# A Fourier mixing layer and a maxout layer: the 96-point stage of batches 2 to 7 as two 48-point ones

## The chip, the cores and the metric

The kernel runs on one core of a Trainium2 chip. A core has five engines with instruction queues of their own: TensorE (matrix products; PE in the profile, its weight loads PEld), VectorE (DVE), ScalarE (ACT), GpSimd (POOL) and SyncE (SP, which here only issues transfers). Sixteen DMA engines move data between device memory, SBUF (on-chip, 128 partitions) and nothing else; TensorE writes to PSUM, from which VectorE and ScalarE copy. The metric is the device time of one execution in microseconds (us); less is better.

## The reference

```python
def _attn_ref(x, filt_r, filt_i):              # x: 8 x 3072 x 256, float32
    X = np.fft.rfft(x, axis=1)
    F = (filt_r + 1j * filt_i)[None, :, :]     # 1537 x 256
    Y = X * F
    y = np.fft.irfft(Y, n=x.shape[1], axis=1)
    return y.astype(np.float32)

def _moe_ref(x, w1, w2, w_out):                # 24576 tokens, 256 -> 1024 -> 256
    h1 = x @ w1
    h2 = x @ w2
    g = np.maximum(h1, h2)
    return (g @ w_out).astype(np.float32)
```

The second function is applied to the first one's output, with batch and sequence flattened.

## The kernel before

**The transform.** The 3072 points of a batch are taken as 96 rows (p) of 32 (m). Stage one, `f1` (L277), is a 96-point real transform over the rows: TensorE multiplies the table `C1` (96x96) with `x` for two values of m at a time (512 columns), ScalarE copies the result `pa` from PSUM to a tile `at` (L285), and every second call SP writes `at` to device memory `ad` (L287). `f1_read` (L289) reads `ad` back in another layout as `bt`, in two halves by frequency group. Stage two is made in *visits* (L333): visit n multiplies four groups with 64x64 tables `U` (`s2`, L301, results `px`), VectorE multiplies `px` by the filter `F` (`product`, L310, result `pq`, two of them per visit), and the next visit takes `pq` back through 64x64 tables `VP` and `VQ` (`s3`, L316, results `pz`), which ScalarE copies to `zt` (L327) and SP writes to device memory `zd` (L328). A batch has seven visits: the first has only `s2`, the last only `s3`. The 64x64 tables use the array as four tiles: two row halves by two column halves. `z_read` (L295) reads `zd` back as `zr` in two halves. `s4` (L342) is the 96-point inverse, which gives `y`, 384 tokens at a time; ScalarE and VectorE copy one `py` each.

**The maxout layer.** max(h1, h2) is computed as h2 + relu(h1 - h2): `Wd` = w1 - w2 and `M` = w2 w_out are made at the start. For a tile of 384 tokens, `moe_h` (L361) makes one of eight blocks `ph` of the hidden layer, whose relu goes to `gt` by ScalarE (L371) or VectorE (L369), and `moe_o` (L382) makes three or four matmuls of the output of the tile before it, `po`. VectorE copies two finished `po` to `ot` (L406) and Pool issues the output transfers (L380).

**The order.** The whole order is written out by hand: each engine executes its instructions in the order in which the program issues them. After a start section (batch 0's transform, weights, tables) the main loop runs over 65 tiles with eight steps each, so 64 steps are one batch of output. A step is `moe_h`, then three or four matmuls of `moe_o`, then what was planned for this step, in the order of the `plan` calls (L562). After step 4 of a tile (6 in the last of a batch) comes `s4` of the next tile. While batch b's output is made, the visits of batch b + 1 run (`plan_f2`, L570), `f1` of batch b + 2 (`plan_f1`, L565, every third step) and the loads of x for batch b + 3 (`plan_x`, L576). While batch 0's output is made, `f1` of both batch 1 (steps 4 to 19) and batch 2 (20 to 27, 54 to 61) run, and batch 1's visits stand at steps 28, 32, 36, 39, 42, 46 and 49.

**Buffers.** All results of `f1`, `s2`, `s3`, `s4` and `moe_h` go through one PSUM tag, `ps`, with six buffers (L66) that are handed out in strict turn: a new tile waits until the tile six before it has been read. `po` has a tag of its own with two. `bt` and `zr` have two buffers, `at` four (of four m each), x sixteen.

**Queues.** Pool loads x with a cast to bf16 (`load_x`, L75) and issues the output transfers. SP issues `ad`, `bt`, `zd` and `zr`. Each queue executes in order, and a transfer whose data is not ready holds those behind it.

Of the kernel before, what the change touches and what calls it, by code (L numbers as in the profile page):

```python
# [8 lines left out]
FP32 = mybir.dt.float32  # L9
BF16 = mybir.dt.bfloat16  # L10
AF = mybir.ActivationFunctionType
OP = mybir.AluOpType

B = 8
N = 3072
D = 256
HID = 1024
NP = 96
NM = 32
NW = 12  # L20
NU = 24
# [5 lines left out]
def kernel(  # L27
# [14 lines left out]
    nc = tc.nc  # L42
    V, S, G, TE = nc.vector, nc.scalar, nc.gpsimd, nc.tensor

    const = ctx.enter_context(tc.tile_pool(name="const", bufs=1))
    C1 = const.tile([NP, 96], BF16)
# [13 lines left out]
    w2T = const.tile([128, 8, D], BF16)  # L60

    dram = ctx.enter_context(tc.tile_pool(name="dram", bufs=2, space=bass.MemoryType.DRAM))
    xpool = ctx.enter_context(tc.tile_pool(name="xpool", bufs=16))
    bpool = ctx.enter_context(tc.tile_pool(name="bpool", bufs=2))
    pqpool = ctx.enter_context(tc.tile_pool(name="pqpool", bufs=6))
    ps = ctx.enter_context(tc.tile_pool(name="ps", bufs=6, space=bass.MemoryType.PSUM))  # L66
# [6 lines left out]
    xb = {}  # L73

    def load_x(b, c):  # L75
        t_ = xpool.tile([NP, 4, D], BF16, tag="xb", name="xb")
        src = x[b].rearrange("(p m) d -> p m d", m=NM)
        G.dma_start(out=t_, in_=src[:, 4 * c:4 * c + 4, :])  # L78
        xb[b, c] = t_

    def load_f(h):
# [63 lines left out]
    def table_c():  # L145
        p96 = init.tile([128, 1], FP32)
        V.tensor_scalar(p96, pid, 1.0 / 96.0, None, OP.mult)
        uc = init.tile([NP, 48, 2], FP32)
        rc = init.tile([NP, 48, 2], FP32)
        kf = kc.rearrange("p w g s -> p (w g s)")  # L150
        V.tensor_scalar(uc[:, :, 0], kf, p96[0:NP], 0.25, OP.mult, OP.add)
        V.tensor_scalar(uc[:, :, 1], kf, p96[0:NP], None, OP.mult)
        V.tensor_scalar(uc[:, 0:1, 1], pid[0:NP], 0.5, 0.25, OP.mult, OP.add)
        V.tensor_scalar(rc, uc, RND, RND, OP.add, OP.subtract)
        V.tensor_tensor(uc, uc, rc, OP.subtract)
        S.activation(C1, uc.rearrange("p k r -> p (k r)"), AF.Sin, bias=zero[0:NP], scale=TWO_PI)

    ua = init.tile([128, NU, 2, 2, 16], FP32)
    ru = init.tile([128, NW, 64], FP32)
# [111 lines left out]
    bt = {}  # L271
    zr = {}
    ad = {}
    zd = {}
    at_ = {}

    def f1(b, c):  # L277
        if c == 0:
            ad[b] = dram.tile([96, NM, D], BF16, tag="ad", name="ad")
        if c % 2 == 0:  # L280
            at_[b] = apool.tile([96, 4, D], BF16, tag="at", name="at")
        at = at_[b]
        pa = ps.tile([96, 2, D], FP32, tag="ps", name="pa")
        TE.matmul(pa, C1, xb[b, c // 2][:, 2 * (c % 2):2 * (c % 2) + 2], start=True, stop=True)  # L284
        S.activation(at[:, 2 * (c % 2):2 * (c % 2) + 2], pa, AF.Copy)  # L285
        if c % 2 == 1:
            nc.sync.dma_start(out=ad[b][:, 2 * c - 2:2 * c + 2], in_=at)  # L287

    def f1_read(b):  # L289
        bt[b] = bpool.tile([128, NU, D], BF16, tag="bt", name="bt")  # L290
        for h in range(2):
            src = ad[b].rearrange("(u q) m d -> (q m) u d", q=4)[:, 12 * h:12 * h + 12]
            nc.sync.dma_start(out=bt[b][:, 12 * h:12 * h + 12], in_=src)

    def z_read(b, h):  # L295
        if h == 0:
            zr[b] = zrpool.tile([96, NM, D], BF16, tag="zr", name="zr")
        nc.sync.dma_start(out=zr[b][48 * h:48 * h + 48],
                          in_=zd[b][12 * h:12 * h + 12].rearrange("u (q m) d -> (u q) m d", q=4))

    def s2(b, v):  # L301
        px = [ps.tile([128, 2, D], FP32, tag="ps", name="px%d" % s) for s in range(2)]
        for i in range(2):
            for s, g in ((0, 0), (1, 1), (0, 1), (1, 0)):
                u = 2 * (2 * v + i) + g
                TE.matmul(px[s][64 * g:64 * g + 64, i], U[64 * s:64 * s + 64, u], bt[b][64 * s:64 * s + 64, u],  # L306
                          start=True, stop=True)
        return px

    def product(E, v, s, px):  # L310
        pq = pqpool.tile([128, 2, 2, D], BF16, tag="pq", name="pq")
        E.tensor_tensor(pq, px.rearrange("p (o i) d -> p o i d", o=1).to_broadcast([128, 2, 2, D]),  # L312
                        F[:, :, 2 * v:2 * v + 2, s], OP.mult)
        return pq

    def s3(b, v, pq):  # L316
        if v == 0:
            zd[b] = dram.tile([NU, 128, D], BF16, tag="zd", name="zd")
        pz = [ps.tile([128, 2, D], FP32, tag="ps", name="pz%d" % g) for g in range(2)]
        for i in range(2):  # L320
            for q, tab in enumerate((VP, VQ)):
                for g, s in ((0, 0), (1, 1), (0, 1), (1, 0)):
                    TE.matmul(pz[g][64 * s:64 * s + 64, i], tab[64 * g:64 * g + 64, 2 * v + i, s],  # L323
                              pq[s][64 * g:64 * g + 64, q, i], start=(q == 0), stop=(q == 1))
        zt = zpool.tile([128, 2, 2, D], BF16, tag="zt", name="zt")
        for g in range(2):
            S.activation(zt[:, :, g], pz[g], AF.Copy)  # L327
        nc.sync.dma_start(out=zd[b][4 * v:4 * v + 4].rearrange("u p d -> p u d"),  # L328
                          in_=zt.rearrange("p i g d -> p (i g) d"))

    pend = {}

    def visit(b, n):  # L333
        if n > 0:
            s3(b, n - 1, pend.pop((b, n - 1)))
        if n < 6:
            px = s2(b, n)
            pend[b, n] = [product(V, n, s, px[s]) for s in range(2)]

    yt = {}  # L340
# [20 lines left out]
    def moe_h(tt, j):  # L361
        if j == 0:
            gt[tt] = gpool.tile([128, 8, 384], BF16, tag="gt", name="gt")
        y_ = yt[tt]
        ph = ps.tile([128, 384], FP32, tag="ps", name="ph")
        for dc in range(2):
            TE.matmul(ph, Wd[:, dc, 128 * j:128 * j + 128], y_[:, dc], start=(dc == 0), stop=(dc == 1))  # L367
        if (tt, j) in on_v if tt < 8 else j in (1, 3, 6):
            V.tensor_scalar(gt[tt][:, j], ph, 0.0, None, OP.max)  # L369
        else:  # L370
            S.activation(gt[tt][:, j], ph, AF.Relu)  # L371
# [106 lines left out]


    table_c()  # L480
    V.tensor_scalar(I128, cid, pid, None, OP.is_equal)
    V.tensor_scalar(NI, cid, pid, -1.0, OP.is_equal, OP.mult)
# [65 lines left out]
    t2(0, (V, S))  # L548
    spin(2)
    setup.close()  # L550
    apool = ctx.enter_context(tc.tile_pool(name="apool", bufs=4))
    zpool = ctx.enter_context(tc.tile_pool(name="zpool", bufs=3))
    ypool = ctx.enter_context(tc.tile_pool(name="ypool", bufs=3))
    gpool = ctx.enter_context(tc.tile_pool(name="gpool", bufs=2))
# [7 lines left out]
    def plan(b, step, fn, *a):  # L562
        todo.setdefault((b + step // 64, step % 64), []).append((fn, a))

    def plan_f1(b, nb, steps, read):  # L565
        for c, n in zip(range(16), steps):
            plan(b, n, f1, nb, c)
        plan(b, read, f1_read, nb)

    def plan_f2(b, nb, steps, z0, z1):  # L570
        for n, st in zip(range(7), steps):
            plan(b, st, visit, nb, n)
        plan(b, z0, z_read, nb, 0)
        plan(b, z1, z_read, nb, 1)

    def plan_x(b, nb, steps):  # L576
        for c, n in zip(range(8), steps):
            plan(b, n, load_x, nb, c)

    plan(0, 2, t2, 1, (V,))  # L580
    plan(0, 5, prep_t, 0)
    plan(0, 6, prep_t, 1)
    plan(0, 7, prep_m)
    for c in range(2, 8):
        plan(0, 8 * (c - 2) + 8, t2, c, (V,))
    plan_x(0, 2, range(2, 10))
    plan_f1(0, 1, range(4, 20), 20)
    plan_f2(0, 1, (28, 32, 36, 39, 42, 46, 49), 41, 51)
    plan_f1(0, 2, list(range(20, 28)) + list(range(54, 62)), 62)
    plan_x(0, 3, range(54, 102, 6))  # L590
    for b in range(1, B):
        if b + 2 < B:
            plan_f1(b, b + 2, range(1, 64, 3), 54)
        if b + 3 < B:
            plan_x(b, b + 3, range(8, 64, 7))
        if b + 1 < B:
            plan_f2(b, b + 1, range(8, 50, 6) if b == 1 else range(6, 48, 6), 33 if b == 1 else 32, 50 if b == 1 else 49)

    for tt in range(8 * B + 1):
        b, i = divmod(tt, 8)  # L600
        k = 0
        for j in range(8):
            step = 8 * i + j
            if tt < 8 * B:
                moe_h(tt, j)
            if tt > 0:
                n = 3 if j in (3, 7) else 4
                moe_o(tt - 1, k, k + n)
                k += n
            for fn, a in todo.get((b, step), ()):  # L610
                fn(*a)
            if j == (4 if i < 7 else 6) and tt + 1 < 8 * B:
                s4(tt + 1)
# [30 lines left out]
```

## Time and profile before

| what | us |
|---|---|
| three runs, median (lowest, highest) | 519.16 (518.43, 519.32) |
| the profiled execution, its own time | 519.43 |
| its span (first to last instruction) | 517.5 |
| TensorE busy in it (5212 matmuls) | 500.9 |
| VectorE / ScalarE / Pool busy | 325.4 / 313.2 / 165.1 |
| granted TensorE clock, mean | 0.99 |

The costliest groups that the text speaks of (line, engine, operation, out<-in, shape, count, then busy us and mean ns of one; behind the bar the engine's idle time before them and what ended most of it):

```profile
L285 ACT ACTIVATE at<-pa 96x512 bf16<-96x512 f32 x112 | 66.4, 593 | 30.0 <-PE pa L284 27.3
L284 PE MATMUL pa<-xb,C 96*96 96x512 bf16 x112 | 42.7, 382 | 0.7 <-DMA xb<-in_x_dram 0.7
L78 POOL DMA_DIRECT2D xb<-in_x_dram x64 | 33.9, 536 | 5.4 <-DMA xb<-in_x_dram 4.3
L323 PE MATMUL pz<-pq,VP 64*64 64x256 bf16 x336 | 21.9, 281 | 0.0
L306 PE MATMUL px<-bt,U 64*64 64x256 bf16 x384 | 20.0, 278 | 0.2
```

And the transfers (KB each, median us from issue to landing):

```profile
xb<-in_x_dram POOLq DMA_DIRECT2D x64, 192.0 KB, 5.8
ad<-at SPq DMA_DIRECT2D x56, 192.0 KB, 3.5
bt<-ad SPq DMA_DIRECT2D x14, 768.0 KB, 8.6
zd<-zt SPq DMA_DIRECT2D x42, 256.0 KB, 3.5
zr<-zd SPq DMA_DIRECT2D x14, 768.0 KB, 7.7
w1f<-in_moe_w_dram SPq DMA_DIRECT2D x2, 512.0 KB, 5.3
```

A matmul's modelled length holds the latency of the pipeline (382 ns for a pa of 512 columns), so lengths of neighbours overlap and the busy time of a group is more than it adds; the distance from one start to the next is what an instruction takes. Idle time of an engine that is not the bottleneck costs nothing.

### The profile page before, as it was taken

The page shows a single profiled execution, that of the slowest core. Times are in us where ns is not written, and L with a number is a line of the kernel's source. Part 1 is how long each engine was busy: PE and PEld are TensorE (multiplying, and loading weights), DVE is VectorE, ACT ScalarE, POOL GpSimd, SP SyncE. Part 2 cuts the span into 40 slices and gives each one's busy share as a digit, 9 for nine tenths or more (in the row PEclk, how much of TensorE's full clock was granted, in tenths as well). Part 3 has the DMA queues.
Part 4 walks back from the last instruction along what each step waited for, and adds up shares of the span by engine and source line. Part 5 has one row for each costly group of instructions (what it writes and reads, how often), then busy time and mean ns, then how long its engine had stood idle before and what let it go on. Part 6 is the DMA issues. An engine that isn't in the chain of part 4 may idle for free.

```text
span 517.5 us, 12635 instructions
## 1 busy us (share of the span) xinstructions
PE 500.9 (97%) x5212; PEld 364.3 (70%) x5212; DVE 325.4 (63%) x503; ACT 313.2 (61%) x636; POOL 165.1 (32%) x289
## 2 busy tenths in 40 slices
PE   7678999999999999999999999999999999999997
PEld 3445777777777777777777777777777777777775
DVE  7673558547774577547764677557774687554543
ACT  6655667766774577656675576646765455544442
POOL 6887212224323232332323233231222122222220
PEclk9879999999999999999999999999999999999999
DMA  7979973879798577874699577892377426521112
GB/s 124 167 208 179 248 240 127 196 228 246 189 227 239 173 169 162 242 229 119 159 215 230 156 169 176 216 258 96 133 186 195 151 100 146 153 84 72 62 62 82
DMA packets 72635, 88.12 MB, mean 170 GB/s; under 512 B 6561, under 2 KB 52898, under 8 KB 71906
## 3 DMA queue, kind: packets, MB, share of 16 engines
q1 hardware_dynamic: 53218, 47.72, 34.3%
q0 software_dynamic: 19360, 39.60, 31.5%
q8 instruction: 41, 0.67, 0.5%
q14 instruction: 16, 0.13, 0.1%
HBM read 54.53 MB, written 47.19 MB: 197 GB/s over the span
## 4 chain that ended last, share of the span: by engine, by line
PE 89%; DMA 5%; POOL 3%; ACT 1%; DVE 1%; issue 0%; SPq 0%; POOLq 0%
PE ph L367 33%; PE po L394 32%; PE po L392 8%; PE pa L284 5%; PE pz L323 5%; PE py L348 4%; DMA xb<-in_x_dram 2%; PE px L306 2%; DMA w1f<-in_moe_w_dram 1%; DMA F<-in_filt_i_dram 1%; POOL Wd L252 1%; POOL xb L78 1%; POOL F L90 1%; POOL F L87 1%; PE pr L467 1%; DVE pq L312 0%
## 5 line engine op out<-in xcount | busy, mean ns | idle before, releaser
L394 PE MATMUL po<-Wo,gt 128*128 128x256 bf16 x1536 | 260.6, 272 | 0.0
L371 ACT ACTIVATE gt<-ph 128x384 bf16<-128x384 f32 x323 | 157.4, 490 | 117.0 <-PE ph L367 116.0
L380 POOL DMA_DIRECT2D out_dram<-ot x186 | 102.0, 553 | 329.8 <-DVE ot L406 321.0
L394 PEld LDWEIGHTS <-gt 128*128 128x128 bf16 x1536 | 149.7, 97 | 61.7
L369 DVE TENSOR_SCALAR gt<-ph 128x384 bf16<-128x384 f32 x189 | 104.0, 554 | 71.9 <-PE ph L367 65.2
L312 DVE TENSOR_TENSOR pq<-px,F 128x1024 bf16<-128x1024 f32 x92 | 108.4, 1220 | 39.6 <-PE px L306 34.5
L367 PEld LDWEIGHTS <-Wd 128*128 128x128 bf16 x1024 | 94.5, 98 | 29.0 <-issue 7.9
L285 ACT ACTIVATE at<-pa 96x512 bf16<-96x512 f32 x112 | 66.4, 593 | 30.0 <-PE pa L284 27.3
L406 DVE COPY ot<-po 128x512 f32<-128x512 f32 x95 | 65.3, 687 | 30.4 <-PE po L394 29.3
L327 ACT ACTIVATE zt<-pz 128x512 bf16<-128x512 f32 x84 | 45.6, 594 | 24.6 <-PE pz L323 24.6
L284 PE MATMUL pa<-xb,C 96*96 96x512 bf16 x112 | 42.7, 382 | 0.7 <-DMA xb<-in_x_dram 0.7
L78 POOL DMA_DIRECT2D xb<-in_x_dram x64 | 33.9, 536 | 5.4 <-DMA xb<-in_x_dram 4.3
L348 PE MATMUL py<-G,zr 96*128 96x96 bf16 x512 | 32.6, 206 | 0.2
L348 PEld LDWEIGHTS <-zr 96*128 96x128 bf16 x512 | 27.7, 98 | 6.1 <-issue 3.1
L323 PE MATMUL pz<-pq,VP 64*64 64x256 bf16 x336 | 21.9, 281 | 0.0
L323 PE MATMUL pz<-pq,VQ 64*64 64x256 bf16 x336 | 20.9, 269 | 0.0
L306 PE MATMUL px<-bt,U 64*64 64x256 bf16 x384 | 20.0, 278 | 0.2
L323 PEld LDWEIGHTS <-VP 64*64 64x64 bf16 x336 | 9.7, 105 | 8.7 <-issue 8.4
L284 PEld LDWEIGHTS <-C 96*96 96x96 bf16 x112 | 13.8, 123 | 2.3 <-DMA xb<-in_x_dram 1.1
L477 PE MATMUL pd<-W 128*128 128x512 bf16 x33 | 11.0, 448 | 1.8 <-DVE zero L123 1.5
L306 PEld LDWEIGHTS <-U 64*64 64x64 bf16 x384 | 10.2, 108 | 2.5 <-issue 2.3
L323 PEld LDWEIGHTS <-VQ 64*64 64x64 bf16 x336 | 9.8, 107 | 0.0
(419 smaller groups left out, 568.3 us busy)
## 6 DMA issues: line engine op xcount, KB each, us to landing
out_dram<-ot POOLq DMA_DIRECT2D x186, 128.0 KB, 2.8
xb<-in_x_dram POOLq DMA_DIRECT2D x64, 192.0 KB, 5.8
ad<-at SPq DMA_DIRECT2D x56, 192.0 KB, 3.5
bt<-ad SPq DMA_DIRECT2D x14, 768.0 KB, 8.6
zd<-zt SPq DMA_DIRECT2D x42, 256.0 KB, 3.5
zr<-zd SPq DMA_DIRECT2D x14, 768.0 KB, 7.7
w1f<-in_moe_w_dram SPq DMA_DIRECT2D x2, 512.0 KB, 5.3
w2f<-in_moe_w_dram SPq DMA_DIRECT2D x2, 512.0 KB, 5.8
```

Source lines behind the costliest of these rows:

```text
L284: TE.matmul(pa, C1, xb[b, c // 2][:, 2 * (c % 2):2 * (c % 2) + 2], start=True, stop=True)
L285: S.activation(at[:, 2 * (c % 2):2 * (c % 2) + 2], pa, AF.Copy)
L312: E.tensor_tensor(pq, px.rearrange("p (o i) d -> p o i d", o=1).to_broadcast([128, 2, 2, D]), F[:, :, 2 * v:2 * v + 2, s], OP.mult)
L323: TE.matmul(pz[g][64 * s:64 * s + 64, i], tab[64 * g:64 * g + 64, 2 * v + i, s], pq[s][64 * g:64 * g + 64, q, i], start=(q == 0), stop=(q ...
L327: S.activation(zt[:, :, g], pz[g], AF.Copy)
L348: TE.matmul(py[:, m], zr[b][:, 4 * i + m, 128 * dc:128 * dc + 128], G1, start=True, stop=True)
L367: TE.matmul(ph, Wd[:, dc, 128 * j:128 * j + 128], y_[:, dc], start=(dc == 0), stop=(dc == 1))
L369: V.tensor_scalar(gt[tt][:, j], ph, 0.0, None, OP.max)
L371: S.activation(gt[tt][:, j], ph, AF.Relu)
L380: E.dma_start(out=dst, in_=ot[tt // 2][:, 3 * (tt % 2) + c])
L394: TE.matmul(p_, g_[:, n - 2, blk], Wo[:, n - 2], start=False, stop=(n == 9))
L406: V.tensor_copy(ot[tt // 2][:, e - 1:e + 1], po[0])
```

## The change

From batch 2 on, stage one is split by the parity of the rows' upper half: with rows p and p + 48 added and subtracted, the 96-point transform becomes a 48-point one of the sums (even frequencies) and one of the differences (odd ones). SP loads x as it is, float32, with rows p and p + 48 side by side on 48 partitions, two m on partitions 0 to 47 and two on 64 to 111 (`load_xf`). Pool makes sums and differences of a quad of four m (`fold`), in bf16. TensorE multiplies them with `CT`, two 64x64 tables on each half of the partitions, as four 64x64 matmuls of 512 columns (`s1`), and ScalarE copies two tiles of 128x512. The `at` tile holds eight m, so there are two writes of 192 KB per two quads (for batch 1, one of 384 KB per four `f1`). `bt` is read in halves by parity, which are halves of its partitions.

The quads of batch b + 2 stand inside the visits of batch b + 1, after `s2`. A visit now stands between `moe_h` and `moe_o` of its step. Batch 1's visits move to steps 28, 31, 34, 38, 42, 46, 49 and 54: an eighth one takes two quads alone, and the first takes none. In later batches the first visit takes two quads and the others one each, at steps 7, 14, 18, 24, 31, 38, 42 (batch 2's) or 0, 7, 14, 18, 24, 31, 38. A load is planned 18 steps ahead of its quad and the fold 10 (22 and 14 for the first quad).

```diff
+    CT = const.tile([128, 2, 64], BF16)
+    XF = [const.tile([128, 2, 2, D], FP32, name="XF%d" % k) for k in range(3)]
-    xpool = ctx.enter_context(tc.tile_pool(name="xpool", bufs=16))
+    xpool = ctx.enter_context(tc.tile_pool(name="xpool", bufs=10))
...
+    def load_xf(b, c):
+        src = x[b].rearrange("(h p m) d -> p h m d", h=2, m=NM)
+        for g in range(2):
+            nc.sync.dma_start(out=XF[c % 3][64 * g:64 * g + 48], in_=src[:, :, 4 * c + 2 * g:4 * c + 2 * g + 2, :])
+
+    def fold(b, c):
+        t_ = xpool.tile([128, 2, 2, D], BF16, tag="xb", name="xsd")
+        f = XF[c % 3]
+        G.tensor_tensor(t_[:, 0], f[:, 0], f[:, 1], OP.add)
+        G.tensor_tensor(t_[:, 1], f[:, 0], f[:, 1], OP.subtract)
         xb[b, c] = t_
...
+    def table_ct():
+        for f in XF:
+            G.memset(f, 0.0)
+        G.memset(CT, 0.0)
+        for g in range(2):
+            G.tensor_copy(CT[64 * g:64 * g + 48, :, 0:48].rearrange("p s (u r) -> p s u r", r=2),
+                          C1[0:48].rearrange("p (u s r) -> p s u r", s=2, r=2))
...
     def f1(b, c):
-        if c % 2 == 0:
-            at_[b] = apool.tile([96, 4, D], BF16, tag="at", name="at")
+        if c % 4 == 0:
+            at_[b] = apool.tile([128, 8, D], BF16, tag="at", name="at")
...
-        if c % 2 == 1:
-            nc.sync.dma_start(out=ad[b][:, 2 * c - 2:2 * c + 2], in_=at)
+        if c % 4 == 3:
+            nc.sync.dma_start(out=ad[b][:, 2 * c - 6:2 * c + 2], in_=at[0:96])
...
+    def s1(b, c):
+        if c == 0:
+            ad[b] = dram.tile([96, NM, D], BF16, tag="ad", name="ad")
+        if c % 2 == 0:
+            at_[b] = apool.tile([128, 8, D], BF16, tag="at", name="at")
+        at = at_[b]
+        pa = [ps.tile([128, 2, D], FP32, tag="ps", name="pa%d" % g) for g in range(2)]
+        for g, r in ((0, 0), (1, 1), (0, 1), (1, 0)):
+            TE.matmul(pa[g][64 * r:64 * r + 64], CT[64 * g:64 * g + 64, r], xb[b, c][64 * g:64 * g + 64, r],
+                      start=True, stop=True)
+        for g in range(2):
+            m0 = 4 * (c % 2) + 2 * g
+            S.activation(at[:, m0:m0 + 2], pa[g], AF.Copy)
+        if c % 2 == 1:
+            for r in range(2):
+                nc.sync.dma_start(out=ad[b][48 * r:48 * r + 48, 4 * c - 4:4 * c + 4], in_=at[64 * r:64 * r + 48])
+
+    def s1_read(b):
+        bt[b] = bpool.tile([128, NU, D], BF16, tag="bt", name="bt")
+        for r in range(2):
+            src = ad[b][48 * r:48 * r + 48].rearrange("(u r) m d -> (r m) u d", r=2)
+            nc.sync.dma_start(out=bt[b][64 * r:64 * r + 64], in_=src)
...
-    def visit(b, n):
-        if n > 0:
+    def visit(b, n, quads):
+        if 0 < n < 7:
             s3(b, n - 1, pend.pop((b, n - 1)))
         if n < 6:
             px = s2(b, n)
+        if b + 1 < B:
+            for c in quads:
+                s1(b + 1, c)
+        if n < 6:
             pend[b, n] = [product(V, n, s, px[s]) for s in range(2)]
...
-    apool = ctx.enter_context(tc.tile_pool(name="apool", bufs=4))
+    apool = ctx.enter_context(tc.tile_pool(name="apool", bufs=2))
...
+    mid = {}
+
+    def plan_f2(b, steps, quads):
+        for n, st in enumerate(steps):
+            mid.setdefault((b, st), []).append((visit, (b + 1, n, quads[n])))
+        plan(b, steps[3] + 4, z_read, b + 1, 0)
+        plan(b, steps[6] + 4, z_read, b + 1, 1)
+        if b + 2 < B:
+            for n, st in enumerate(steps):
+                for c in quads[n]:
+                    lead = 4 * (c == 0 and 1 in quads[n])
+                    plan(b, st - 18 - lead, load_xf, b + 2, c)
+                    plan(b, st - 10 - lead, fold, b + 2, c)
+            plan(b, steps[-1] + 4, s1_read, b + 2)
...
+    plan(0, 3, table_ct)
...
-    plan_x(0, 2, range(2, 10))
     plan_f1(0, 1, range(4, 20), 20)
-    plan_f2(0, 1, (28, 32, 36, 39, 42, 46, 49), 41, 51)
-    plan_f1(0, 2, list(range(20, 28)) + list(range(54, 62)), 62)
-    plan_x(0, 3, range(54, 102, 6))
...
+    plan_f2(0, (28, 31, 34, 38, 42, 46, 49, 54), ((), (0,), (1,), (2,), (3,), (4,), (5,), (6, 7)))
+    two = ((0, 1), (2,), (3,), (4,), (5,), (6,), (7,))
+    plan_f2(1, (7, 14, 18, 24, 31, 38, 42), two)
+    for b in range(2, B - 1):
+        plan_f2(b, (0, 7, 14, 18, 24, 31, 38), two)
...
             if tt < 8 * B:
                 moe_h(tt, j)
+            for fn, a in mid.get((b, step), ()):
+                fn(*a)
             if tt > 0:
```

More of the change, by code (lines that the diff above doesn't have):

```diff
@@ L78, in load_x @@
         G.dma_start(out=t_, in_=src[:, 4 * c:4 * c + 4, :])
+        xb[b, c] = t_
+    def load_xf(b, c):
[7 more added lines that the diff above has]
+        G.tensor_tensor(t_[:, 1], f[:, 0], f[:, 1], OP.subtract)
         xb[b, c] = t_
@@ L284, in f1 @@
         TE.matmul(pa, C1, xb[b, c // 2][:, 2 * (c % 2):2 * (c % 2) + 2], start=True, stop=True)
-        S.activation(at[:, 2 * (c % 2):2 * (c % 2) + 2], pa, AF.Copy)
-        if c % 2 == 1:
-            nc.sync.dma_start(out=ad[b][:, 2 * c - 2:2 * c + 2], in_=at)
+        S.activation(at[0:96, 2 * (c % 4):2 * (c % 4) + 2], pa, AF.Copy)
+        if c % 4 == 3:
+            nc.sync.dma_start(out=ad[b][:, 2 * c - 6:2 * c + 2], in_=at[0:96])
     def f1_read(b):
@@ L568, in plan_f1 @@
         plan(b, read, f1_read, nb)
[L570 to L578, printed above, removed]
+    mid = {}
[11 more added lines that the diff above has]
+            plan(b, steps[-1] + 4, s1_read, b + 2)
     plan(0, 2, t2, 1, (V,))
+    plan(0, 3, table_ct)
     plan(0, 5, prep_t, 0)
@@ L585 @@
         plan(0, 8 * (c - 2) + 8, t2, c, (V,))
-    plan_x(0, 2, range(2, 10))
     plan_f1(0, 1, range(4, 20), 20)
-    plan_f2(0, 1, (28, 32, 36, 39, 42, 46, 49), 41, 51)
-    plan_f1(0, 2, list(range(20, 28)) + list(range(54, 62)), 62)
-    plan_x(0, 3, range(54, 102, 6))
[L591 to L597, printed above, removed]
+    plan_f2(0, (28, 31, 34, 38, 42, 46, 49, 54), ((), (0,), (1,), (2,), (3,), (4,), (5,), (6, 7)))
[3 more added lines that the diff above has]
+        plan_f2(b, (0, 7, 14, 18, 24, 31, 38), two)
     for tt in range(8 * B + 1):
```

## The prediction

> **What bounds the kernel now.** I read the page's totals first, then the windows, then TensorE's timeline around one visit of the 32-point stages, then VectorE's, SP's and Pool's rows there.
>
> ```profile
> PE 500.9 (97%) x5212; PEld 364.3 (70%) x5212; DVE 325.4 (63%) x503; ACT 313.2 (61%) x636; POOL 165.1 (32%) x289
> 200.00:250.00 50.00, 49.95 (x485) 36.75 (x484) 31.95 (x48) 30.87 (x64) 14.67 (x27) 1.00 0.77 194
> ```
>
> The first line is the page's; the second is the window from 200 to 250 us (length, then busy PE, PEld, DVE, ACT, POOL, then clock, DMA share, GB/s). TensorE has 0.05 us of idle in 50 at full clock; the others have a third or more free. So in the main part the end is TensorE's instruction stream, and an edit is worth what it takes from or puts into that stream.
>
> ```profile
> 251.00 0.38 PE L394 MATMUL po<-Wo,gt 128*128 128x256 bf16 x2
> 251.31 0.30 PE L323 MATMUL pz<-pq,VP 64*64 64x256 bf16 x4
> 251.44 0.28 PE L323 MATMUL pz<-pq,VQ 64*64 64x256 bf16 x4
> 251.55 0.28 PE L323 MATMUL pz<-pq,VP 64*64 64x256 bf16 x4
> 251.66 0.28 PE L323 MATMUL pz<-pq,VQ 64*64 64x256 bf16 x4
> 251.77 0.39 PE L306 MATMUL px<-bt,U 64*64 64x256 bf16 x8
> 252.09 0.50 PE L367 MATMUL ph<-y__4370,Wd 128*128 128x384 bf16 x2
> 252.43 0.60 PE L394 MATMUL po<-Wo,gt 128*128 128x256 bf16 x4
> 252.86 0.38 PE L284 MATMUL pa<-xb,C 96*96 96x512 bf16 x1
> 253.08 0.49 PE L367 MATMUL ph<-y__4370,Wd 128*128 128x384 bf16 x2
> ```
>
> Start, modelled length, instruction. Starts are the price, lengths hold pipeline latency. Four 64x64 matmuls of 256 columns start every 0.11 us, so the four lie side by side. One 96x512 pa takes 0.22 (252.86 to 253.08). Entering the 64x64 tiling costs 0.10 (two po of 0.11 end at 251.21, pz starts at 251.31), leaving it as much (px ends at 251.99, ph starts at 252.09). ph and four po take 0.33 and 0.435, one step.
>
> **TensorE's own time.** Batches 2 to 7 lose 6 x 16 = 96 pa at 0.22: 21.1 us. They gain 6 x 8 = 48 quads of four 64x64 matmuls with 512 columns; two groups of 256 columns take 0.215, so 10.3 us. They lie inside visits that pay for the tiling already, but batch 0 gets an eighth visit, 0.2. Sum: 10.6 us off. Bounds of a quad: 0.215 if the four run side by side, 0.43 if only two do (nothing gained). I take 0.215, the px row's behaviour, which has the same four row and column halves.
>
> **What the other engines get.** ScalarE copies pa as before: 16 copies of 512 columns a batch, 0.59 each (its at row), on 128 rows in place of 96. VectorE gets nothing. Pool loses 48 issues of 0.536 (26 us) and gains 96 folds of 128x512. No such fold is in the trace; the nearest rows are Wd's subtraction (2370 ns for 1024 columns) and Pool's pq (2125), so 1.06 to 1.19 each, about 110 us. Pool ends near 250 of 518 us and stays covered. Four pq of VectorE ran beside Pool's, and all 92 lie between 1214 and 1226 ns, so I add nothing for the two engines together. Pool's queue also issues the output DMAs (L380), which wait for VectorE's ot 321 us in total; a fold that waits for x would hold them, but two ot tiles hold 32 steps' output.
>
> x now goes through SP: 96 loads of 192 KB, ahead of which stand zd and ad writes (waiting for ScalarE), and bt and zr reads (waiting for those writes). Nearest landings: 3.5 us (ad, 192 KB) and 5.3 (w1f, fp32, 512 KB). A load is planned 8 steps before its fold, the fold 10 steps before its matmuls; a step is 59.2/64 = 0.92 us (visits 245.75 and 304.92 of two batches), so 16 us cover load, queue and a 2.3 us pair of folds. Cost zero; without that cover each late quad stops TensorE, and the output DMAs with it. Price bounds: 0 to 2 us in each of the six batches.
>
> **Where time comes back: the PSUM ring.** Tag ps has six buffers in strict turn, so a tile waits for the tile six before it. A visit now takes six in a row (pz, pz, px, px, pa, pa), or in the first visit of a batch px, px and four pa. The next ph then needs the first of them.
>
> ```profile
> 233.73 0.41 PE L306 MATMUL px<-bt,U 64*64 64x256 bf16 x8
> 234.19 2.36 DVE L312 TENSOR_TENSOR pq<-px,F 128x1024 bf16<-128x1024 f32 x2 [0.23 <-PE px L306]
> 245.96 1.08 ACT L327 ACTIVATE zt<-pz 128x512 bf16<-128x512 f32 x2 [0.51 <-PE pz L323]
> ```
>
> The first two lines are a batch's first visit (PE, DVE); the third is ScalarE in the visit whose px starts at 245.75. Counting from px's start, the products free px0 at 0.46 + 1.22 = 1.68 and px1 at 2.82; I add 0.04 for the signal. First visit with two quads: px 0.22, quads to 0.65, leave 0.75, four po to 1.18; ph wants px0's buffer and waits 0.54, runs 0.77 with its po, and at 2.48 the next ph waits 0.38 for px1's. Together 0.91; at step 7 of batch 1 only three po stand between, 0.1 more. Five batches: 4.65 us. The other visits: zt frees pz0 at 0.86 and ph comes at 0.97 (0.86 where three po stand between): no wait. The last pa tile takes the buffer of the ph just before the visit, whose relu ends at 0.20, and starts at 0.22: no wait, by a hair. At step 18 two ph and then two py follow; the second py comes at 2.56 and needs px1's buffer at 2.85: 0.27, in five batches and at steps 34 and 42 of batch 0: 1.9 us. Sum 6.55; bounds 4 (signals earlier, py's wait covered) and 9 (0.1 in each of some 25 ordinary visits more).
>
> **Where time comes back: batches 0 and 1.**
>
> ```profile
> 66.70 1.18 SPq L293 DMA_DIRECT2D bt<-ad  x2
> 101.05 0.32 SPq L298 DMA_DIRECT2D zr<-zd  x1
> 111.88 1.18 SPq L293 DMA_DIRECT2D bt<-ad  x2
> 108.49 0.50 PE L348 MATMUL py<-G,zr 96*128 96x96 bf16 x8
> ```
>
> SP's issues, and the py that waits for zr. (a) bt of batch 1: issued at 66.70, the quicker half lands 4.4 later (bt's shortest), px starts at 72.8. Eight pa fewer stand before that visit (1.76 us), and the last ad write is 384 KB in place of 192, up to 1 us more (192 KB in 3.5, 512 in 5.3): I take 0.7, bounds 0 and 2. (b) zr of batch 1 landed 7.3 after its issue, at 108.35, and py started at 108.49: no slack. TensorE now comes 1.76 - 0.22 - 0.63 (quad 5; the eighth visit) = 0.9 sooner, and two ad writes and two x loads stand before zr on SP, 0.3: I take 1.1, bounds 0 and 3 (longest zr landing 9.3). (c) bt of batch 2 is now split by partitions, so the first px needs both halves. From step 49's pz (96.06) zr lands at 12.6, the last ad 0.6 later, bt 7 us after that (6.2 and 8.4 are median and longest there): 20.3. TensorE is there at 117.2 - 96.06 - 0.8 (one step earlier) - 2.4 (eleven pa) + 0.85 + 1.1 = 19.9: 0.4, bounds 0 and 2.5. Sum 2.2. From batch 1 on bt is asked for some 20 steps ahead, which covers its median landing of 8.6.
>
> **Sum.** -10.6 + 6.55 + 2.2 = -1.85. The profiled execution took 519.43 (span 517.5), 0.27 above the median of 519.16. Forecast of the median: 517.3.
>
> The Trainium skill, TensorEngine Tiling (Array Packing), section PSUM Bottleneck, says that tiling quickens TensorE but not the emptying of PSUM, which may become the bound. That speaks against this change. The trace before does not show it (TensorE has no idle time at its visits); the second rival is what its full force would do here.
>
> **Rivals.**
> 1. The waits stay small: all 10.6 kept but for the products of the first visits (say 3) and 1 to 3 at the start: 513.5. For it: VectorE and ScalarE are a third idle. Against: the ring's turns are fixed, and px1 is free at 2.82 in each batch alike.
> 2. Copies out of PSUM pace every visit. Some 30 ordinary visits have margins of 0.02 to 0.1; if ScalarE is one relu (0.49) late, as after a step whose relu, y and at come together, ph waits 0.3 to 0.4 in each: 9 to 12 us on top, 526 to 529; in a third of them 521. It decides from the point where pz0 is freed later than 0.97 after px's start. Slower.
> 3. Reads late from batch 1 on: bt's longest landing is 14.3, and last ad, bt and x loads now share SP's queue. With step 38's copies at 2.8 and the write at 6.5, bt would land at 20.8 when TensorE arrives at about 20.5; each 2 us of x traffic ahead costs that in five batches: 523 to 527. Against: bt's median of 8.6 leaves 5 us.
> 4. The change doesn't bring the side by side work: quads at 0.43, no saving, all waits kept: 528. Against: the px row.
>
> **Chances.** About 0.2% (1 us) is what a measurement can tell from no change. Forecast 0.40 (own range 515.5 to 519.5; 0.30 of it below 518.1, 0.10 within 1 us of 519.16). Rival 1: 0.21, faster. Rival 2: 0.18 and rival 3: 0.15, slower but for 0.03. Rival 4: 0.06, slower. So faster 0.51, same 0.13, slower 0.36. The range takes most of rival 1 and the milder thirds of 2 and 3: 511.5 to 523.
>
> **What would show it.** Four pa starts within 0.01 us and the next group 0.21 later: the quad's price. ph after a batch's first visit starting 1.72 and 2.86 after px: the ring. py at step 62 of batch 0 and px at step 7 of batch 1 waiting for DMA: the joint. TensorE waits on pa for Pool's xsd, or on ph for ScalarE in ordinary visits, would make the prediction wrong, as would any longer pq beside a fold.

## The result, and the profile after

| | before | after |
|---|---|---|
| median (lowest, highest), us | 519.24 (518.43, 519.32) | 553.92 (550.33, 554.71) |
| the profiled execution / its span | 519.43 / 517.5 | 554.71 / 552.9 |
| granted TensorE clock, mean | 0.99 | 0.954 |
| Pool busy, us | 165.1 | 262.1 |

The ratio of the times is 1.066 (95% interval 1.061 to 1.071): slower by 34.7 us, outside the range of 511.5 to 523. The page of the changed kernel, TensorE's totals and its two rows of the 40 slices (13.8 us each):

```profile
PE 508.6 (92%) x5304; PEld 368.2 (67%) x5308; DVE 326.0 (59%) x503; ACT 312.9 (57%) x636; POOL 262.1 (47%) x343
PE   7578989969999699988999699997999999999997
PEclk9989989987999699997999989997999999999999
```

TensorE was 97% busy and is 92% busy, and the idle time is not spread: behind the start section the dips (6, 6, 8 and 8, 6, 7) stand 60 to 70 us apart, about the length of a batch, and beside them the granted clock dips too. A window between two of those places (length, then busy PE, PEld, DVE, ACT, POOL, clock, DMA share, GB/s) looks as the forecast wanted it:

```profile
200.00:240.00 40.00, 40.00 (x437) 30.13 (x436) 26.34 (x40) 26.38 (x54) 19.29 (x26) 1.00 0.73 189
```

No idle time, full clock. So all of the loss lies where one batch's visits end and the next one's begin. What TensorE waits for there, from the view of waits (total us, times, longest), with one row of Pool and two medians of the transfers:

```profile
POOL xsd L91 <- DMA XF<-in_x_dram: 47.5, 7, 10.7
PE pa L326 <- POOL xsd L91: 10.3, 7, 3.0
PE px L352 <- DMA bt<-ad: 8.4, 3, 3.2
PE pa L326 <- POOL xsd L92: 5.1, 7, 0.8
PE py L398 <- DMA zr<-zd: 2.5, 1, 2.5
```

```profile
bt<-ad SPq DMA_DIRECT2D x14, 768.0 KB, 11.3
XF<-in_x_dram SPq DMA_DIRECT2D x96, 192.0 KB, 4.5
```

Read the list from its end to its source: pa waits for a fold, the fold waits for x, up to 10.7 us at once, though x's loads land after 4.5 us in the median. One joint in order of time shows how. SP, Pool and TensorE around the first visit of batch 5 (L339 is the read of `bt`, L344 that of `zr`, L86 the load of x, L91 and L92 the fold):

```profile
294.35 0.30 SPq L344 DMA_DIRECT2D zr<-zd  x1
296.03 1.85 SPq L339 DMA_DIRECT2D bt<-ad  x2
297.93 10.28 SPq L86 DMA_DIRECT2D XF<-in_x_dram  x6
```

```profile
313.41 1.26 POOL L91 TENSOR_TENSOR xsd<-XF 128x512 bf16<-128x512 f32 x1 [10.67 <-DMA XF<-in_x_dram]
...
317.07 1.26 POOL L92 TENSOR_TENSOR xsd<-XF 128x512 bf16<-128x512 f32 x1
```

```profile
311.25 0.48 PE L352 MATMUL px<-bt,U 64*64 64x256 bf16 x8
314.72 0.37 PE L326 MATMUL pa<-xsd,CT 64*64 64x512 bf16 x1 [2.98 <-POOL xsd L91]
...
318.38 0.64 PE L326 MATMUL pa<-xsd,CT 64*64 64x512 bf16 x3 [0.64 <-POOL xsd L92]
318.95 0.61 PE L442 MATMUL po<-M,y__5021 128*128 128x256 bf16 x2
```

The first load for quad 0 is issued 3.6 us behind `zr` and 1.9 behind `bt`, that is behind 2.3 MB; its issue alone holds SP for 7.9 us (0.43 in the median of the 96), and it lands 14.3 us after its issue, at 312.26. TensorE is at the visit at 311.25. Then four folds of 1.22 us stand one behind the other, and TensorE, between them, does one or three matmuls at a time. It goes on with the maxout layer at 318.95, 7.7 us after the visit began; px, two quads and the way out of the tiling have a price of 0.75. The windows of the load's way and of the visit:

```profile
294.00:311.00 17.00, 17.00 (x152) 13.24 (x149) 8.69 (x16) 8.15 (x17) 2.64 (x5) 1.00 1.03 244
311.00:315.40 4.40, 1.11 (x11) 0.35 (x10) 2.36 (x2) 0.69 (x2) 1.99 (x2) 1.00 0.59 127
315.40:322.20 6.80, 5.04 (x21) 2.41 (x21) 0.56 (x1) 2.21 (x5) 6.79 (x9) 0.50 0.54 156
```

In the first the DMA engines are full (share 1.03; before, such a stretch has 0.89). In the last the clock is 0.50 for 6.8 us. The same happens at 246 and 377 us, and at 179, where `bt` is late as well: at the first visits of batches 3 to 6, which take the quads of 4 to 7.

**Accounting.** A gap or wait of TensorE, here and below, is the distance from one start to the next less the full-speed price of the first of the two, so it comes out 0.1 to 0.3 us longer than in the profile's rows, and more at half speed. TensorE's gaps of over 0.3 us from 60 us on add up to 35.7 us. The saving by the prediction's prices is 10.6. The span grew by 35.4; 10.3 us are left, which are put down to 44.3 us at half speed (there is none from 32.6 us to the end before). That last term is a remainder, but the trace bears out its size: the smaller distances, of up to 0.3 us above the full-speed price, add up to 34.1 us, 13.9 of them at half speed, against 24.2 us in the kernel before.

### The profile page after: what moved, and what is told of

Same layout as the page of the kernel before. It is cut to its first block, busy times and chain, and to the rows that moved or that the text cites. A ratio compares the mean times of both kernels' runs of the same rounds, so it can differ in the third digit from the quotient of the medians.

```text
span 552.9 us, 13037 instructions
## 1 busy us (share of the span) xinstructions
PE 508.6 (92%) x5304; PEld 368.2 (67%) x5308; DVE 326.0 (59%) x503; ACT 312.9 (57%) x636; POOL 262.1 (47%) x343
## 4 chain that ended last, share of the span: by engine, by line
PE 72%; DMA 13%; POOL 5%; SPq 4%; issue 3%; ACT 2%; DVE 1%; POOLq 0%; ACTq 0%; DVEq 0%
PE po L444 27%; PE ph L417 25%; PE po L442 7%; PE pz L369 4%; DMA XF<-in_x_dram 4%; DMA ad<-at 3%; SPq L86 3%; PE py L398 3%; DMA bt<-ad 3%; PE pa L326 2%; DMA xb<-in_x_dram 2%; PE px L352 2%; POOL xsd L92 1%; POOL Wd L274 1%; POOL xsd L91 1%
## 5 line engine op out<-in xcount | busy, mean ns | idle before, releaser
L444 PE MATMUL po<-Wo,gt 128*128 128x256 bf16 x1536 | 267.9, 278 | 0.0
L417 PEld LDWEIGHTS <-Wd 128*128 128x128 bf16 x1024 | 98.4, 100 | 14.6 <-issue 0.9
L91 POOL TENSOR_TENSOR xsd<-XF 128x512 bf16<-128x512 f32 x48 | 61.1, 1272 | 57.2 <-DMA XF<-in_x_dram 47.5
L456 DVE COPY ot<-po 128x512 f32<-128x512 f32 x95 | 65.2, 687 | 35.4 <-PE po L444 34.3
L330 ACT ACTIVATE at<-pa 128x512 bf16<-128x512 f32 x96 | 52.2, 606 | 26.0 <-PE pa L326 26.0
L92 POOL TENSOR_TENSOR xsd<-XF 128x512 bf16<-128x512 f32 x48 | 60.9, 1268 | 0.0
L326 PE MATMUL pa<-xsd,CT 64*64 64x512 bf16 x192 | 24.8, 421 | 15.4 <-POOL xsd L91 10.3
L398 PEld LDWEIGHTS <-zr 96*128 96x128 bf16 x512 | 29.2, 98 | 5.1 <-DMA zr<-zd 2.7
L326 PEld LDWEIGHTS <-CT 64*64 64x64 bf16 x192 | 9.6, 110 | 21.2 <-issue 15.8
L352 PEld LDWEIGHTS <-U 64*64 64x64 bf16 x384 | 10.6, 109 | 12.1 <-DMA bt<-ad 6.3
L369 PEld LDWEIGHTS <-VP 64*64 64x64 bf16 x336 | 9.7, 105 | 13.3 <-issue 13.3
L307 ACT ACTIVATE at<-pa 96x512 bf16<-96x512 f32 x16 | 9.5, 596 | 4.6 <-PE pa L306 4.1
## 6 DMA issues: line engine op xcount, KB each, us to landing
bt<-ad SPq DMA_DIRECT2D x14, 768.0 KB, 11.3
```

The source lines that it names most:

```text
L91: G.tensor_tensor(t_[:, 0], f[:, 0], f[:, 1], OP.add)
L92: G.tensor_tensor(t_[:, 1], f[:, 0], f[:, 1], OP.subtract)
L330: S.activation(at[:, m0:m0 + 2], pa[g], AF.Copy)
L398: TE.matmul(py[:, m], zr[b][:, 4 * i + m, 128 * dc:128 * dc + 128], G1, start=True, stop=True)
L444: TE.matmul(p_, g_[:, n - 2, blk], Wo[:, n - 2], start=False, stop=(n == 9))
L456: V.tensor_copy(ot[tt // 2][:, e - 1:e + 1], po[0])
```

## The experiments

The kernel before measured 519.1 to 519.3 us beside all of them; diffs are against the changed kernel unless it says otherwise, ratios to the kernel before. Theory 1 came first: x's loads come behind `zr` and `bt` on SP, and the folds, late, stop TensorE.

### The first three quads' loads ahead of the reads

```diff
-                    plan(b, st - 18 - lead, load_xf, b + 2, c)
+                    first = steps[0] if quads[0] else None
+                    early = first is not None and c < 3
+                    plan(b, (first - (28 if b > 1 else 25)) if early else st - 18 - lead, load_xf, b + 2, c)
```

> The change with one thing moved: the x loads of a batch's first three quads are issued at step 36 (46 in batch 0), ahead of the reads of zr and bt on SP's queue, and not behind them at steps 42 to 53. Theory 1 (the loads stand behind 2.3 MB of zr and bt reads on SP's queue, so the folds of quads 0 and 1 start when TensorE is already there): the waits of pa for xsd at the first visit of batches 3 to 7 (each 5 to 7 us, and about 7 us of half clock behind it) go; what is left are the waits for bt and zr: 518 to 528. Rival A (Pool is too slow for the folds, 1.2 us each, wherever the loads stand): 545 or more, pa still waits for xsd. Rival B (bt itself is late at each first visit and would hold TensorE anyway): 535 to 548, the wait moves from pa to px.

Measured: 522.10 us (519.13 to 524.68), ratio 1.005 (1.003 to 1.008), as theory 1 expected. 31.8 us come back from issuing six transfers per batch earlier, ahead of the reads. SP, and then TensorE's first visit of batch 5:

```profile
270.71 3.01 SPq L86 DMA_DIRECT2D XF<-in_x_dram  x6
280.73 0.30 SPq L344 DMA_DIRECT2D zr<-zd  x1
281.13 1.74 SPq L339 DMA_DIRECT2D bt<-ad  x2
```

```profile
296.69 0.41 PE L352 MATMUL px<-bt,U 64*64 64x256 bf16 x7 [0.38 <-DMA bt<-ad]
296.83 0.70 PE L326 MATMUL pa<-xsd,CT 64*64 64x512 bf16 x8
```

The eight pa run in a row, and no pa waits for `xsd` anywhere. What is left is 13.0 us of waits: 2.08 us at 70, 6.21 at 108 (`zr`, whose second read is issued at 108.5, in the changed kernel at 105.0), 1.98 at 124, 2.10 at 178 and 0.65 at 296.

### x's loads issued by Pool

```diff
-            nc.sync.dma_start(out=XF[c % 3][64 * g:64 * g + 48], in_=src[:, :, 4 * c + 2 * g:4 * c + 2 * g + 2, :])
+            G.dma_start(out=XF[c % 3][64 * g:64 * g + 48], in_=src[:, :, 4 * c + 2 * g:4 * c + 2 * g + 2, :])
```

> The change with the x loads issued by Pool instead of SP, same type, same steps. Theory 1 (SP's order is what makes them late): the loads land in about 6 us as x did before, the waits of pa for xsd go or fall below 1 us: 518 to 530. Rival A (Pool's time): Pool gets 96 more issues of about 0.5 us and the wait for xsd grows: 555 or more. Rival C (the DMA engines have no room for float32 x, whoever issues it): landings stay above 10 us, 545 to 556.

Measured: 553.89 us (552.77 to 555.42), ratio 1.067 (1.064 to 1.070): nothing gained, a miss for theory 1. Its waits and transfers:

```profile
PE px L352 <- DMA bt<-ad: 30.1, 9, 6.4
```

```profile
XF<-in_x_dram POOLq DMA_DIRECT2D x96, 192.0 KB, 5.2
bt<-ad SPq DMA_DIRECT2D x14, 768.0 KB, 14.3
```

x is in time (10.2 us at the longest), pa no longer waits, and `bt` is late in its place: its median goes from 11.3 to 14.3 us. So SP's order decides only who is late. `zr`, `bt` and the first quads of x don't all get through the DMA engines between step 38 and the first visit (share 1.05 from 296 to 316 us, by the windows). This is theory 2: TensorE's saving is real, and what is lost is transfers that land too late where batches meet, whichever queue they are on. Rival C's total came true, its late x did not: the median landing is 5.2 us.

### `bt` in four parts

```diff
         for r in range(2):
-            src = ad[b][48 * r:48 * r + 48].rearrange("(u r) m d -> (r m) u d", r=2)
-            nc.sync.dma_start(out=bt[b][64 * r:64 * r + 64], in_=src)
+            src = ad[b][48 * r:48 * r + 48].rearrange("(u r) m d -> (r m) u d", r=2)[:, 12 * h:12 * h + 12]
+            nc.sync.dma_start(out=bt[b][64 * r:64 * r + 64, 12 * h:12 * h + 12], in_=src)
```

(with `for h in range(2):` around it)

> The change with bt read in four parts, first both partition halves of the first twelve frequency groups, then of the last twelve, so that the first visits need half of the bytes. Theory 1: the waits of px for bt (2.7 to 3.5 us at 70 (unchanged read), 121 and 179 us) shrink at 121 and 179, the waits of pa for xsd stay: 545 to 554. Rival B (the halves by partitions are the main cause): 530 or less.

Measured: 545.82 us (543.07 to 547.62), ratio 1.051 (1.046 to 1.055), as expected. The wait of px at 121 us falls from 3.46 to 0.87 us, the one at 179 goes, and pa's waits stay (13.7 us here, 5.9 more for L92):

```profile
PE pa L326 <- POOL xsd L91: 13.7, 7, 5.4
```

### x loaded and folded once

```diff
-            TE.matmul(pa[g][64 * r:64 * r + 64], CT[64 * g:64 * g + 64, r], xb[b, c][64 * g:64 * g + 64, r],
+            TE.matmul(pa[g][64 * r:64 * r + 64], CT[64 * g:64 * g + 64, r], xb[2, c][64 * g:64 * g + 64, r],
...
-                for c in quads[n]:
+                for c in quads[n] if b == 0 else ():
```

> The change without the loads and folds of batches 3 to 7, whose quads take batch 2's sums and differences (so five batches of x are left out of the work). Theory 1: no wait for xsd and bt quicker, since nothing but ad, zd, zr and bt is on SP's queue: what is left of the change's loss is batch 0 and 1 (waits of 2.7, 2.6 and 3.5 us and their half clock, some 14 us), so 512 to 518. Rival D (the order in the visits or the PSUM buffers cost TensorE time without any wait for x): 520 or more, with waits of ph behind the first visits. The ring as I had forecast it would show here as waits of 0.5 and 0.4 us of the two ph behind a batch's first visit.

Measured: 520.74 us (518.73 to 523.60), ratio 1.003 (1.001 to 1.005). After 176 us TensorE has no gap over 0.3 us, with the same PSUM turns and the same visits. The loads and folds of batches 3 to 7, and what they push back, cost 33.2 us, then. The total missed the expected 512 to 518 by its other part: the joint of batches 0 and 1, where the waits are 2.73 us at 70, 1.44 at 109, 3.91 at 118 and 1.62 at 175, with 6.8 us at half speed. Against 519.29 - 10.6 = 508.7 this leaves 12.0 us for them; 12.0 and 33.2 make up the 34.7 + 10.6 that were lost.

### Early loads and four parts together

The edits of the first and the third experiment in one kernel.

> The early loads and bt in four parts together, batch 2 still the new way. Theory 2: the waits of px at 124 and 178 us (2.0, 2.1) and 296 (0.65) of the run with early loads go; those at 70 (bt of batch 1, unchanged read, 2.1) and 108 (zr, 6.2, with about 7 us of half clock) stay: 516 to 520. If the parts do not help: 521 to 523.

Measured: 517.36 us (514.77 to 520.40), ratio 0.997 (0.995 to 0.999), as expected. Two waits are left, 1.86 us at 71 and 5.60 us at 109, the latter for `zr`, with 6.8 us at half speed behind it. Batch 2 the new way with this read of `zr` ahead of the early loads was not tried.

### Batch 2 the old way

Early loads and four parts, and in the joint of batches 0 and 1 the order of before: batch 2 by 96-point matmuls, x cast on Pool's queue, batch 1's visits at their old steps.

```diff
-            plan(b, steps[-1] + 4, s1_read, b + 2)
+            if b:
+                plan(b, steps[-1] + 4, s1_read, b + 2)
...
-    plan_f2(0, (28, 31, 34, 38, 42, 46, 49, 54), ((), (0,), (1,), (2,), (3,), (4,), (5,), (6, 7)))
+    for c, n in enumerate((2, 3, 6, 8, 10, 12, 14, 16)):
+        plan(0, n, load_x, 2, c)
+    plan_f2(0, (28, 32, 36, 39, 42, 46, 49), ((),) * 7)
+    plan_f1(0, 2, list(range(20, 28)) + list(range(54, 62)), 62)
...
-    plan_f2(1, (7, 14, 18, 24, 31, 38, 42), two)
+    plan_f2(1, (8, 14, 18, 24, 31, 38, 42), two)
```

(left out: the early loads' and four parts' lines as above, batch 3's early loads at 39 - 2c steps ahead, and `table_ct` at step 30 in place of 3)

> The change kept for batches 3 to 7 alone: batch 2 goes the old way (x with a cast by Pool, 96-point f1 in batch 0's steps, bt in frequency halves, batch 1's visits at the old steps), x of the first three quads is loaded ahead of the zr and bt reads, and bt from batch 3 on is read in four parts. Theory 2 (the saving of TensorE is real, 1.75 us a batch; all that was lost are transfers that land too late at the joints, and the half clock behind them): five batches save 8.8 us, no wait over 0.5 us is left: 510 to 513. Rival D (the visits themselves cost time): 515 or more without waits for transfers.

Measured: 511.81 us (510.50 to 514.26), ratio 0.987 (0.985 to 0.989), as expected and faster than both kernels. One of its windows, with the first visit of batch 6 in it (at 340 us):

```profile
300.00:350.00 50.00, 50.00 (x528) 37.51 (x528) 32.15 (x48) 32.48 (x66) 26.67 (x33) 1.00 0.83 226
```

Joint included, TensorE has no idle time and full clock. 7.3 us are gained; five sixths of the forecast's 10.6 would be 8.8.

### The folds made twice

The kernel with early loads, and `for _ in range(2):` around fold's two instructions, which gives the same sums and differences.

> The early loads, with every fold made twice (Pool gets some 115 us more). Theory 2: Pool's rate isn't the bound: 520 to 525, as with the early loads alone (522.1). Rival A: pa waits for xsd again, 530 or more.

Measured: 544.26 us (543.75 to 545.41), ratio 1.049 (1.048 to 1.050), against 522.10 with single folds: rival A's time and wait, and a miss for the theory that Pool has this to spare.

```profile
PE pa L327 <- POOL xsd L93: 6.0, 8, 0.8
PE pa L327 <- POOL xsd L92: 4.6, 3, 3.3
```

Pool is busy for 379.1 us of 541.9, 70%, and yet pa waits 11 times. Single folds are not the bound (no such wait with early loads), but a second 2.5 us per quad already is. The share of Pool's busy time doesn't tell this: a fold stands behind Pool's output transfers, which wait for `ot`, and has to come in the few steps between its load and its visit.

### The kernel before with `bt` split by partitions

Against the kernel before; nothing else is changed:

```diff
-            src = ad[b].rearrange("(u q) m d -> (q m) u d", q=4)[:, 12 * h:12 * h + 12]
-            nc.sync.dma_start(out=bt[b][:, 12 * h:12 * h + 12], in_=src)
+            src = ad[b].rearrange("(u g q) m d -> g (q m) u d", g=2, q=2)[h]
+            nc.sync.dma_start(out=bt[b][64 * h:64 * h + 64], in_=src)
```

> The kernel before, with bt read in halves by partitions instead of frequency groups, nothing else changed. Theory 2: the parts land as late as before, the second about 8 us after its issue in batches 1 and 2, and px needs both: waits of about 2.0 us at 73 and 3.5 us at 117 and some half clock, none later: 524 to 529. Rival B (partition halves make the read itself slower): the second part lands 11 us or more after its issue there, 530 or more.

Measured: 532.96 us (531.83 to 533.51), ratio 1.027 (1.025 to 1.028); theory 2 expected 524 to 529, rival B's account held (10.9 us for the longest landing where it said 11 or more). The landings of `bt` up to 125 us (before, then this kernel; min/median/max):

```profile
DMA to landing us min/median/max: 4.4/6.2/8.4
```

```profile
DMA to landing us min/median/max: 6.5/8.0/10.9
```

Two losses in one edit: the first px needs both halves in place of one, and each half lands later. The waits of px are 4.27 us at 72 and 6.56 at 122, and each is followed by 6.8 us at half speed.

### Frequency halves on all partitions, in the changed kernel

```diff
-                nc.sync.dma_start(out=ad[b][48 * r:48 * r + 48, 4 * c - 4:4 * c + 4], in_=at[64 * r:64 * r + 48])
+                dst = ad[b].rearrange("(u g q) m d -> g u q m d", g=2, q=2)[r][:, :, 4 * c - 4:4 * c + 4]
+                nc.sync.dma_start(out=dst, in_=at[64 * r:64 * r + 48])
...
+    s1_read = f1_read
```

> The change with bt read as before the change: the 48-point results are written to ad in the row order of f1, and bt is read in two halves of the frequency groups, each onto all 128 partitions. Nothing else is changed, so the x loads still stand behind zr and bt. Theory 3 (halves by partitions cost twice: px needs both, and each part lands later, 6.5 us for the first in batch 1 and 2 against 4.4 and 4.8 with all partitions): bt's first half lands about 2 us sooner and px no longer waits for the second: the waits of px at 122 and 180 us fall below 1.5 us, x behind bt lands some 2 us sooner; pa still waits for xsd at batches 3 to 7's first visits: 535 to 546. If only the need for both halves counted, as with four parts: 544 to 548.

Measured: 534.58 us (533.53 to 538.93), ratio 1.030 (1.028 to 1.032), 19.3 us less than the changed kernel and a little below the expected range. px's wait at 119 us is 0.60 (3.46) and none is left at 180; pa's waits for `xsd` are still 12.3 us (15.4). The edit changes the writes of `ad` along with the read. The read's shape and x's lateness are two costs.

### The same halves with batch 2 the old way

The kernel of 511.81 us with these halves in place of the four parts.

> Batch 2 the old way, x of the first three quads early, and bt of batches 3 to 7 in frequency halves on all partitions (as in the run before) in place of four parts. Theory 2: no wait was left with four parts but 0.5 and 0.7 us in batches 0 and 1, so the same time, 510 to 513; bt's first part lands 1 to 2 us sooner without anybody waiting for it.

Measured: 512.17 us (510.73 to 512.72), ratio 0.987 (0.985 to 0.989): no difference from the other, as expected. The waits of px at 73 and 117 us are 1.47 and 0.89 us (0.48 and 0.70 with four parts); behind them, with x early, either shape of read is covered.

## Why the prediction was wrong, point by point

**TensorE's own time: right.** An ordinary visit of the changed kernel:

```profile
284.20 0.39 PE L352 MATMUL px<-bt,U 64*64 64x256 bf16 x8
284.42 0.39 PE L326 MATMUL pa<-xsd,CT 64*64 64x512 bf16 x4
284.74 0.50 PE L444 MATMUL po<-Wo,gt 128*128 128x256 bf16 x3
```

Four pa of 512 columns start together; po follows 0.32 us later, which is the 0.215 of the forecast and 0.10 for leaving the tiling. Rival 4 falls with it.

**The step that failed: "16 us cover load, queue and a 2.3 us pair of folds. Cost zero", bounded by "0 to 2 us in each of the six batches".** At each of the four first visits that take quads 0 and 1 of batches 4 to 7, TensorE lost 5.8 to 7.2 us (2.9 of them for `bt` in the first of the four), and the half clock besides; with x early (522.10 us) all of this went but waits for `bt` of 2.1 us at the first of them and 0.65 at the third. The step took the load by "nearest landings" of 3.5 and 5.3 us, medians of transfers in other places. It named `zr` and `bt` as standing ahead on SP, and priced neither. And it counted a pair of folds, 2.3 us, where a first visit takes two quads, four folds in series: 4.9. The 22 steps from the plan to the visit are some 20 us; the load came to be issued 13.3 us before the visit, landed after 14.3, and 4.9 us of folds came on top. The run on Pool's queue adds that the order on SP is not the whole of it: moved past it, x is in time and `bt` is not. "From batch 1 on bt is asked for some 20 steps ahead, which covers its median landing" fails with it: for the first of the four visits, at 179.5 us, the second half of `bt` was issued 12.0 us ahead and landed after 14.8. In company with x and `zr` the median is 11.3 us, and the joint has to be judged by what lands there.

**Batches 0 and 1: right places, wrong size.** Forecast were 0.7, 1.1 and 0.4 us; measured 2.73 us at px of batch 1, 2.63 at py, 3.46 at px of batch 2, 8.8 in place of 2.2, and the half clock. In the last, the forecast counted that px needs both halves, but took each half's landing as before; the run of the kernel before with that split shows them 1.8 to 2.5 us later (shortest, median and longest). The read was also issued late there: the last write of `ad`, issued at 107.1 us, took 8.5 us to land, against 3.4 in the median, and `bt` waited for it.

**The PSUM ring: its rule was wrong.** "Six buffers in strict turn", which the description of the kernel has too, was read from the code, counted in the order of the visit's calls, and not tested on any wait of the trace before. That trace contradicts it:

```profile
135.35 0.39 PE L306 MATMUL px<-bt,U 64*64 64x256 bf16 x8
135.79 2.36 DVE L312 TENSOR_TENSOR pq<-px,F 128x1024 bf16<-128x1024 f32 x2 [1.59 <-PE px L306]
...
137.66 0.49 PE L367 MATMUL ph<-y__2438,Wd 128*128 128x384 bf16 x2
```

Between the second px and this ph lie ph, ph, pa, py and py, so that px is the tile six before it. Yet ph starts at 137.66 us, while VectorE reads that px until 138.14. From 60 to 480 us 14 ph do so. The forecast's waits behind a first visit are not there either. The visit of batch 6 in the kernel of 511.81 us:

```profile
340.06 0.41 PE L353 MATMUL px<-bt,U 64*64 64x256 bf16 x8
340.52 2.36 DVE L359 TENSOR_TENSOR pq<-px,F 128x1024 bf16<-128x1024 f32 x2 [0.77 <-PE px L353]
...
340.77 0.11 PEld L326 LDWEIGHTS <-CT 64*64 64x64 bf16 x3 [0.36 <-ACT gt L422]
...
341.56 0.49 PE L418 MATMUL ph<-y__6096,Wd 128*128 128x384 bf16 x2
```

The next ph starts 1.50 us after px (forecast 1.72), before VectorE is done with the first px, at 341.74. A smaller wait stands in its place: the weights of the last pa wait for the relu of the ph just before the visit (the row at 340.77), and that pa starts 0.25 us late, in four of the five first visits of this kernel. The forecast had looked at this turn in the other visits alone ("no wait, by a hair"), where up to 0.06 us shows. 6.55 us were forecast for the ring, and about 1.0 is found at the first visits; in the fastest version all that is missing against 8.8 us is 1.5. In which order the buffers are handed out instead is not shown, and a price of the clock alone was not tried.

**The engines: Pool about right, its margin not.** Folds take 1.27 us (forecast 1.06 to 1.19), Pool is busy for 262.1 us (forecast near 250), and VectorE's pq lies between 1214 and 1226 ns as before. "Stays covered" is true of the share alone, as the doubled folds show.

**The rivals.** Rival 3 came nearest to the mechanism (last ad, `bt` and x share SP's queue, reads late from batch 1 on) and had 523 to 527 us. But it had x delaying `bt`, where in most places `zr` and `bt` delayed x, and it priced a late read by its lateness alone, without the serial folds and the clock. Rival 2, copies out of PSUM, is not there: the longest wait of an ordinary visit for one is the 0.06 us above. Rival 1's 513.5 is near what the change brings when its transfers are planned anew. No term of the sum, and no rival, held the clock.

## What to carry to other kernels

Price a moved transfer at the place where it goes: list what is outstanding at its issue, add the bytes up against what that stretch of the trace moves per us, and follow the chain through to the consumer, with all of its serial steps. A median landing is no bound for the joint where three large reads meet. And where TensorE is the bound, give each wait of over two microseconds a second price for the clock.

## What the hardware showed unasked

**The clock.** Half speed comes in stretches of 3.4, 6.8 and 10.2 us, and follows waits of TensorE. In these runs, from 60 us on, single waits of up to 2.08 us were followed by none; of those from 2.1 to 3.0 us some were, for 3.4 us (2.10, 2.63, 2.72, and one of 2.73), and some not (2.20, 2.42, 3.00, and another of 2.73); waits of 3.2 us or more were all followed by 3.4 to 10.2 us, and so were most groups of several in a row (not one of 1.33 and 1.16 us in the run with doubled folds). The windows around one, in the kernel with early loads, after a wait of 2.10 us at 177.6:

```profile
177.50:180.60 3.10, 1.27 (x19) 0.60 (x19) 0.48 (x1) 0.75 (x3) 2.34 (x2) 1.00 0.60 192
180.60:184.00 3.40, 3.40 (x16) 2.11 (x15) 2.38 (x4) 2.27 (x5) 0.00 (x0) 0.50 0.24 56
```

TensorE is busy all through the second, at 0.50. The Trainium skill, TensorE: Matmul & The Clock Gate, section "What's actually happening", has a free-running window of some 3.4 us and the half clock after an idle window; the lengths here agree, but a wait of 2.10 us, well under a window, was enough.

**An issue that holds its queue.** SP's issue of a 192 KB load takes 0.43 us in the median and took 7.9 behind `zr` and `bt` (6.0 to 6.3 at the three other joints), so a full stretch delays not only the landing but every issue behind it.

**Halves by partitions.** A 768 KB read into 64 partitions landed in 6.5 us at the least, into 128 partitions in 4.4. The Trainium skill, SBUF — State Buffer, section "Door 1: The DMA port swizzle (why `[64,N]` ≈ `[32,N]`)", says that 64 partitions on one side reach only half of the ports; the direction agrees, the loss here is a factor of 1.5.
